# First four projection blocks run token block by token block, with matmuls on zeros before the first ones

## The chip, the cores and the metric

The kernel runs on one core of a Trainium2 chip. A core has five engines, each with its own instruction stream that it works off in program order: TensorE (PE, matrix products; its weight loads are listed as PEld), VectorE (DVE), ScalarE (ACT), GpSimd (POOL) and SyncE (SP, which here only issues DMA transfers and waits before them where the data isn't ready). Matmuls write to PSUM; everything else is in SBUF or in DRAM. The metric is the device time of the core in microseconds (us).

## The reference

```python
def mha(x, wqkv, wo):                       # x: 1 x 2048 x 512, 32 heads of 16
    q, k, v = split_heads(x @ wqkv)         # wqkv: 512 x 1536
    p = softmax(einsum("bhqd,bhkd->bhqk", q, k) * 16 ** -0.5)
    o = einsum("bhqk,bhkd->bhqd", p, v)
    return merge_heads(o) @ wo              # wo: 512 x 512

x = A_x
g = sigmoid((x * gate_w).sum(-1, keepdims=True))
return g * mha(x, A_wqkv, A_wo) + (1 - g) * mha(x, B_wqkv, B_wo)
```

Two attention blocks work on the same x with weights of their own, and a gate for each token mixes their results. Everything is float32.

## The kernel before

The kernel has a prologue, which projects x to queries, keys and values of both attention blocks, and a main loop over 64 heads (32 of each), which computes scores, exponentials and weighted sums. The change is in the prologue alone.

**The projection of queries and keys.** x comes in transposed (`xT`, 512 features by 2048 tokens) and is loaded in four token blocks of 512 (`load_x`). Each is split into a high and a low part in the format float32r (`split_x`: a cast on ACT to `xh`, a subtraction on DVE to `xl`). There are 16 projection blocks, `blocks`: for each attention block and each of four groups of eight heads, one for the queries and one for the keys, with weights of 512 x 128. A block's weights are loaded by `load_w` into one of three `wraw` buffers and split by `split_w` like x (`whi`, `wlo`, two buffers each). A product is then three products of parts (high by high, low by high, high by low) of four matmuls each: 12 matmuls for a block and 512 tokens, each 128x128 by 128x512.

**`project_qk`** takes one block and goes over two halves of 1024 tokens. A half is 24 matmuls into one of two PSUM tiles `ps_pro`; ACT then copies the result out as the high part `part0`, DVE makes the low part `part1` by a subtraction, and two stores on SP write them to DRAM (`qd` or `kd`). For a block of keys the difference of the first two blocks of 512 keys is computed on POOL too, split and stored (`key_difference`). After each half `between()` may put in score matmuls of the first heads.

**The order.** It is written out by hand: every engine gets its instructions in the order in which the Python code names them. At the start (lines 276 to 283) come the weights of block 0 and the first token block of x in four pieces, both are split, and then token blocks 1 to 3 are loaded and split in two pieces each, with the loads of the weights of blocks 1 and 2 between. The loop over the blocks (lines 296 to 311) splits the weights of the next block, issues the load of the weights of the block three further on, loads the value weights at block 2 and splits them at block 4, and projects. Then, at block 7, the values of the first attention block are projected (`project_v`), and later the heads' stacks of queries and keys are loaded back from DRAM (`load_stacks`).

SP issues all the transfers of the prologue but the load of the values; a store whose data isn't ready holds up the issues written behind it. ACT and DVE wait in the same way.

Of the kernel before, what the change touches and what calls it, by code (L numbers as in the profile page):

```python
# [23 lines left out]
F32 = mybir.dt.float32  # L24
F32R = mybir.dt.float32r
BF = mybir.dt.bfloat16
AF = mybir.ActivationFunctionType
ALU = mybir.AluOpType
# [4 lines left out]
P = 128  # L33
S = 2048
DM = 512
# [3 lines left out]
KC = DM // P  # L39
NQ = S // 512  # L40
# [7 lines left out]
HALVES = (0, 64)  # L48
SC = 3 * DH
KS = S + 512  # L50


@with_exitstack
def gated_mha(ctx: ExitStack, tc: tile.TileContext, xT, x, wqkv_a, wo_a, wqkv_b, wo_b, gate_w, out):
    nc = tc.nc
    pe, act, dve, pool = nc.tensor, nc.scalar, nc.vector, nc.gpsimd
# [6 lines left out]
    ps_m = ctx.enter_context(tc.tile_pool(name="ps_m", bufs=3, space=PSUM))  # L63

    qd = [[dram.tile([2, HG, DH, S], F32, name=f"qd{s}{g}") for g in range(NG)] for s in range(2)]
    kd = [[dram.tile([2, HG, DH, KS], F32, name=f"kd{s}{g}") for g in range(NG)] for s in range(2)]
    vd = [dram.tile([S, H * 17], F32, name=f"vd{s}") for s in range(2)]
# [112 lines left out]
    with tc.tile_pool(name="xs", bufs=1) as xs, tc.tile_pool(name="pro", bufs=2) as pro, \  # L180
            tc.tile_pool(name="ps_pro", bufs=2, space=PSUM) as ps_pro, \
            tc.tile_pool(name="ps_x", bufs=1, space=PSUM) as ps_x:
        xh = [xs.tile([P, KC, 512], F32R, name=f"xh{c}") for c in range(NQ)]
        xl = [xs.tile([P, KC, 512], F32R, name=f"xl{c}") for c in range(NQ)]
        wblocks = {}

        raws = {}

        def load_w(s, col, n):
            raw = pro.tile([P, KC, n], F32, name="raw" if n == 512 else "wraw", bufs=2 if n == 512 else 3)  # L190
            nc.sync.dma_start(raw, wqkv[s][:, col:col + n].rearrange("(k p) c -> p k c", p=P))
            raws[s, col] = raw

        def split_w(s, col, n):
            raw = raws.pop((s, col))
            tag, bufs = ("wv", 1) if n == 512 else ("w", 2)
            hi = pro.tile([P, KC, n], F32R, name=f"{tag}hi", bufs=bufs)
            lo = pro.tile([P, KC, n], F32R, name=f"{tag}lo", bufs=bufs)
            act.copy(hi, raw)
            dve.tensor_tensor(lo, raw, hi.bitcast(F32), op=ALU.subtract)  # L200
            wblocks[s, col] = (hi, lo)

        def load_x(c, n):
            raw = pro.tile([P, KC, 512], F32, name="raw")
            for k in range(0, KC, n):
                nc.sync.dma_start(raw[:, k:k + n], xT[k * P:(k + n) * P, c * 512:(c + 1) * 512].rearrange(
                    "(k p) t -> p k t", p=P))
            return raw

        def split_x(c, n, raw):  # L210
            for k in range(0, KC, n):
                act.copy(xh[c][:, k:k + n], raw[:, k:k + n])  # L212
                dve.tensor_tensor(xl[c][:, k:k + n], raw[:, k:k + n], xh[c][:, k:k + n].bitcast(F32),
                                  op=ALU.subtract)

        def key_difference(dst, parts):
            d = [pro.tile([P, 512], F32, name=f"kdiff{i}", bufs=1) for i in range(2)]
            for i in range(2):
                pool.tensor_tensor(d[i], parts[i][:, :512], parts[i][:, 512:], op=ALU.subtract)
            pool.tensor_tensor(d[0], d[0], d[1], op=ALU.add)  # L220
            hi = pro.tile([P, 512], F32R, name="kdiff_hi", bufs=1)
            lo = pro.tile([P, 512], F32R, name="kdiff_lo", bufs=1)
            pool.tensor_copy(hi, d[0])
            pool.tensor_tensor(lo, d[0], hi.bitcast(F32), op=ALU.subtract)
            for i, t in enumerate((hi, lo)):
                nc.sync.dma_start(dst[i].rearrange("h d t -> (h d) t")[:, S:], t.bitcast(F32))

        def project_qk(s, g, isk, between):
            hi, lo = wblocks.pop((s, isk * DM + g * P))
            dst = (kd if isk else qd)[s][g]  # L230
            for half in range(2):
                ps = ps_pro.tile([P, 1024], F32, name="ps_pro")
                for c in range(2):
                    cc = half * 2 + c
                    n = 0
                    for a, b in ((hi, xh[cc]), (lo, xh[cc]), (hi, xl[cc])):
                        for k in range(KC):
                            pe.matmul(ps[:, c * 512:(c + 1) * 512], a[:, k], b[:, k],  # L238
                                      start=n == 0, stop=n == 3 * KC - 1)
                            n += 1  # L240
                pt = [pro.tile([P, 1024], F32R, name=f"part{i}") for i in range(2)]
                act.copy(pt[0], ps)  # L242
                dve.tensor_tensor(pt[1], ps, pt[0].bitcast(F32), op=ALU.subtract)  # L243
                for i in range(2):
                    nc.sync.dma_start(dst[i].rearrange("h d t -> (h d) t")[:, half * 1024:(half + 1) * 1024],
                                      pt[i].bitcast(F32))
                if isk and half == 0:
                    key_difference(dst, [t.bitcast(F32) for t in pt])
                between()

        v_st = [const.tile([P, H, 17], F32, name=f"v_st{i}") for i in range(2)]
        for t in v_st:
            pool.memset(t[:, :, 16:17], 1.0)

        def project_v(s, t):
            hi, lo = wblocks[s, 2 * DM]
            c, o = divmod(t * P, 512)
            last = s == 1 and t == NT - 1
            ps = ps_m.tile([P, 512], F32, name="ps_m") if last else ps_pro.tile([P, 1024], F32, name="ps_pro")
            n = 0  # L260
            for a, b in ((xh[c], hi), (xl[c], hi), (xh[c], lo)):
                for k in range(KC):
                    pe.matmul(ps[:, :DM], a[:, k, o:o + P], b[:, k], start=n == 0, stop=n == 3 * KC - 1)  # L263
                    n += 1
            v = ps[:, :DM].rearrange("p (h d) -> p h d", h=H)
            act.copy(v_st[t % 2][:, :, 0:16], v)  # L266
            nc.sync.dma_start(vd[s][t * P:(t + 1) * P, :], v_st[t % 2].rearrange("p h d -> p (h d)"))

        blocks = [(s, g, isk) for s in range(2) for g in range(NG) for isk in range(2)]

        def block(fn, i):
            if i < len(blocks):
                s, g, isk = blocks[i]
                fn(s, isk * DM + g * P, P)

        block(load_w, 0)
        x0 = load_x(0, 1)
        block(split_w, 0)
        split_x(0, 1, x0)
        for c in range(1, NQ):  # L280
            split_x(c, 2, load_x(c, 2))
            if c < 3:
                block(load_w, c)
        ahead = [(m, part) for m in range(NT + LEAD) for part in range(NQ)]

        def run_ahead(n):
            turn[0] = 0
            for _ in range(n):
                m, part = ahead.pop(0)
                max_part(m, part, ps_x if part == NQ - 1 else None)  # L290
                if (m, part) == (NT - 1, NQ - 1):
                    max_split(0)
                    pending.append(0)

        pending = []
        for i, (s, g, isk) in enumerate(blocks):
            block(split_w, i + 1)
            block(load_w, i + 3)
            if i in (2, 8):
                load_w(i // 8, 2 * DM, DM)  # L300
            if i in (4, 9):
                split_w(i // 8, 2 * DM, DM)
            project_qk(s, g, isk, lambda: run_ahead((i >= 10) + 2 * (i >= 13)))
            if i in (5, 6, 8, 9):
                load_stacks(i // 8, HALVES[(i - 5) % 3:][:1])
            if i == 7:
                for t in range(NT):
                    project_v(0, t)
            if i == 9:
                for c in range(4):  # L310
                    load_v(0, c)
        for t in range(NT):
            project_v(1, t)
            if pending:
                pending[0] += 1
                if pending[0] == 3:
                    max_rows(pending.pop() - 3)
            if t and t != NT - 2:
                run_ahead(4)
        assert not ahead and not pending  # L320
# [233 lines left out]
    pt = {}  # L554
# [70 lines left out]
    for r in range(0, ROUNDS, 2):  # L625
        h, kt = divmod(r, NT)
# [10 lines left out]
        scored, parts = 0, 2  # L637
# [62 lines left out]
```

## Time and profile before

| | us |
|---|---|
| time before, median of the runs | 2811.56 |
| lowest of the runs | 2810.78 |
| the profiled execution's own time | 2810.61 |
| its span, from the first to the last instruction | 2808.8 |
| PE busy | 2789.1 |
| ACT busy | 2416.8 |
| DVE busy | 2397.4 |
| first real matmul starts at | 5.65 |
| projection block 1 starts at | 24.78 |

Rows of the profile name the line of the kernel, the engine, the operation, the tile written and the tiles read with their shapes (partitions x elements). In a list in order of time the first two numbers are the start and the duration in us, "x4" says that four instructions are merged into the row, and the brackets hold the idle time of the engine ahead of it and what ended it. A merged row of pipelined matmuls runs into the next one by the latency of the last, so the pace is read from the starts. A row for a stretch of time lists the length, the busy time of PE, PEld, DVE, ACT and POOL with the number of instructions, the granted clock of TensorE as a share of full speed, the busy share of the 16 DMA engines, and GB/s. "SPq" is an issue of a transfer by SP, not the transfer.

### The profile page before, as it was taken

How to read it: one execution, taken by the hardware profiler on the slowest of the kernel's cores; microseconds unless marked ns; L12 is line 12 of the kernel's file. 1: busy time of each engine (PE TensorE's matmuls, PEld its weight loads, DVE VectorE, ACT ScalarE, POOL GpSimd, SP SyncE). 2: the span in 40 equal slices, each digit the busy share in tenths (PEclk: the TensorE clock that was granted, in tenths of full speed). 3: DMA queues.
4: the chain of work that ended last, by engine and by line, in shares of the span. 5: the costliest groups of instructions: out<-in, count | busy, mean ns of one | idle time of the engine just before them, and what ended most of it. 6: DMA issues, size and time to landing. Idle time of an engine off the chain costs nothing.

```text
span 2808.8 us, 65084 instructions
## 1 busy us (share of the span) xinstructions
PE 2789.1 (99%) x26016; PEld 1429.3 (51%) x26016; DVE 2397.4 (85%) x4395; ACT 2416.8 (86%) x4755; POOL 280.2 (10%) x473
## 2 busy tenths in 40 slices
PE   8999999999999999999999999999999999999999
PEld 6877544444444444444444455544444444445544
DVE  3135899999999999999999878899999999998884
ACT  3221799999999999999999977899999999998785
POOL 3121132000000000000100231000000000011201
PEclk9999999999999999999999999999999999999999
DMA  7683433333333233333432442332333343333302
GB/s 254 208 252 145 93 80 86 56 61 62 73 65 57 52 61 62 60 63 61 92 56 51 107 93 74 61 59 51 65 58 61 62 80 72 57 76 91 77 11 93
DMA packets 86086, 231.62 MB, mean 82 GB/s; under 512 B 22134, under 2 KB 32342, under 8 KB 73238
## 3 DMA queue, kind: packets, MB, share of 16 engines
q1 hardware_dynamic: 83222, 218.53, 35.3%
q0 software_dynamic: 2560, 8.91, 1.2%
q8 instruction: 205, 3.36, 0.5%
q14 instruction: 99, 0.81, 0.1%
HBM read 158.46 MB, written 68.94 MB: 81 GB/s over the span
## 4 chain that ended last, share of the span: by engine, by line
PE 96%; DMA 2%; DVE 1%; SPq 1%; ACT 0%; issue 0%; POOL 0%; DVEq 0%; ACTq 0%
PE acc L566 38%; PE ps_st L615 31%; PE ps_m L124 14%; PE ps_pro L238 5%; PE ps_m L450 3%; PE ps_pro L263 3%; PE ps_st L124 1%; DMA qd<-part 1%; DMA raw<-in_xT 1%; DMA q_st<-qd 0%; DVE mxp L130 0%; DMA rb<-rd 0%; DMA vd<-v_st 0%; PE ps_st L450 0%; PE ps_st L501 0%
## 5 line engine op out<-in xcount | busy, mean ns | idle before, releaser
L617 ACT ACTIVATE p<-ps_st 128x512 f32<-128x512 f32 x4061 | 2131.0, 628 | 132.4 <-PE ps_m L124 71.4
L130 DVE TENSOR_REDUCE mxp<-ps_m 128x1 f32<-128x512 f32 x3072 | 1977.0, 684 | 150.5 <-PE ps_m L124 69.7
L615 PE MATMUL ps_st<-q_st,k_st 50*128 50x512 f32 x4061 | 1353.9, 438 | 0.3 <-ACT excess L139 0.3
L124 PE MATMUL ps_m<-k_st,q_st 48*128 48x512 f32 x3574 | 1265.4, 444 | 1.3 <-DVE mxp L130 0.7
L566 PE MATMUL acc<-p,vg 128*17 128x256 f32 (+2 forms) x16208 | 1187.5, 386 | 3.0 <-DVE ev L574 2.0
L615 PEld LDWEIGHTS ps_st<-q_st,k_st 50*128 50x128 f32 x4061 | 675.0, 184 | 379.6 <-ACT p L617 227.7
L124 PEld LDWEIGHTS ps_m<-k_st,q_st 48*128 48x128 f32 x3574 | 602.3, 184 | 365.1 <-DVE mxp L130 327.1
L566 PEld LDWEIGHTS acc<-p,vg 128*17 128x17 f32 x16208 | 322.7, 96 | 530.4 <-issue 404.4
L146 DVE CUSTOM_DVE_ANT_0 excess<-ps_m,excess 128x512 f32<-128x512 f32 x502 | 341.9, 681 | 0.0
L139 ACT ACTIVATE excess<-ps_st 128x512 f32<-128x512 f32 x502 | 300.7, 599 | 1.2 <-DVE mxp L130 1.2
L155 POOL CAST mparts<-mrow 128x16 fp32r<-128x16 f32 x64 | 12.6, 196 | 2038.1 <-DVE mrow L154 2038.1
L124 PE MATMUL ps_st<-k_st,q_st 48*128 48x512 f32 x502 | 205.2, 409 | 0.0
L242 ACT CAST part<-ps_pro 128x1024 fp32r<-128x1024 f32 x32 | 32.5, 1015 | 133.1 <-PE ps_pro L238 103.7
L243 DVE TENSOR_TENSOR part<-ps_pro,part 128x1024 fp32r<-128x1024 f32 x32 | 39.2, 1225 | 111.1 <-ACT part L242 92.2
L124 PEld LDWEIGHTS ps_st<-k_st,q_st 48*128 48x128 f32 x502 | 92.1, 183 | 0.2 <-issue 0.2
L450 PE MATMUL ps_m<-wo,ot 128*128 128x512 f32 (+1 forms) x354 | 90.7, 401 | 0.0
L266 ACT COPY v_st<-ps_pro 128x512 f32<-128x512 f32 x31 | 18.2, 587 | 79.5 <-PE ps_pro L263 73.7
L238 PE MATMUL ps_pro<-xh,whi 128*128 128x512 f32 x256 | 72.6, 402 | 9.9 <-ACT xh L212 9.1
L450 PEld LDWEIGHTS ps_m<-wo,ot 128*128 128x128 f32 (+1 forms) x354 | 64.0, 188 | 21.1 <-DVE mxp L146 6.8
L238 PE MATMUL ps_pro<-xh,wlo 128*128 128x512 f32 x256 | 69.4, 393 | 0.0
L238 PE MATMUL ps_pro<-xl,whi 128*128 128x512 f32 x256 | 69.1, 392 | 0.0
L238 PEld LDWEIGHTS ps_pro<-xh,whi 128*128 128x128 f32 x256 | 47.4, 190 | 25.1 <-ACT xh L212 11.7
(105 smaller groups left out, 902.3 us busy)
## 6 DMA issues: line engine op xcount, KB each, us to landing
k_st<-kd SPq DMA_DIRECT2D x128, 320.0 KB
q_st<-qd SPq DMA_DIRECT2D x128, 256.0 KB
k_st<-kd SPq DMA_DIRECT2D x128, 160.0 KB
qd<-part SPq DMA_DIRECT2D x32, 512.0 KB
kd<-part SPq DMA_DIRECT2D x32, 512.0 KB
q_st<-qd SPq DMA_DIRECT2D x128, 128.0 KB
od<-ev SPq DMA_DIRECT2D x63, 256.0 KB
vd<-v_st SPq DMA_DIRECT2D x32, 272.0 KB
```

Source lines behind the costliest of these rows:

```text
L124: pe.matmul(ps, q[b:b + SC, t * P:(t + 1) * P], k[b:b + SC, c * 512:(c + 1) * 512], start=True, stop=True)
L130: dve.tensor_reduce(mxp[h][:, t, part:part + 1], ps, op=ALU.max, axis=AX.X)
L139: act.activation(excess[m], ps, AF.Relu)
L146: dve.tensor_tensor_reduce(e, ps, e, 1.0, LOWEST, ALU.add, ALU.max, mxp[h][:, t, 1:2])
L238: pe.matmul(ps[:, c * 512:(c + 1) * 512], a[:, k], b[:, k], start=n == 0, stop=n == 3 * KC - 1)
L242: act.copy(pt[0], ps)
L243: dve.tensor_tensor(pt[1], ps, pt[0].bitcast(F32), op=ALU.subtract)
L263: pe.matmul(ps[:, :DM], a[:, k, o:o + P], b[:, k], start=n == 0, stop=n == 3 * KC - 1)
L450: pe.matmul(ps, ot[a][:n, slot, sl], wt[b][:n, g], start=G == groups[0] and i == 0, stop=G == groups[-1] and i == 2)
L566: pe.matmul(acc[32 * c:32 * c + 17, qa * P:qb * P], v[:, 4 * a + c if final else kt, j], p[:, c * 512 + qa * P:c * 512 + qb * P], start=fi ...
L615: pe.matmul(ps, k[b:b + SC + 2, kk * P:(kk + 1) * P], q[b:b + SC + 2, cc * 512:(cc + 1) * 512], start=True, stop=True)
L617: act.activation(pt[r][:, c * 512:(c + 1) * 512], ps, AF.Exp, scale=SCALE)
```

## The change

`FIRST = 4`: the first four blocks (queries and keys of the first two groups of heads of the first attention block) are no longer projected one after the other. The kernel goes over the four token blocks of x, and in each it projects blocks 0 and 1 into the two halves of one PSUM tile, then blocks 2 and 3. Their split weights stay in SBUF (four buffers for two). The other 12 blocks are projected as before, each in two halves of two token blocks.

The weights of blocks 1 and 2 are loaded between token blocks 0 and 1 of x, those of block 3 behind token block 1; the loads of blocks 4, 5 and 6, and the split of block 4, stand behind the four projected blocks. The value weights are loaded at block 4 and split at block 5. Token block c + 2 of x is loaded and token block c + 1 split after the first pair of token block c. The stores of a pair are four of 512 columns each where there were two of 1024. The key difference is now made from two calls, one for each of the token blocks 0 and 1.

Ahead of each of the first four real matmuls stand 10, 5, 3 and 6 matmuls on a tile of zeros in bf16, into a PSUM tile that is not read.

```diff
-            tag, bufs = ("wv", 1) if n == 512 else ("w", 2)
+            tag, bufs = ("wv", 1) if n == 512 else ("w", FIRST)
...
+        zeros = pro.tile([P, 512], BF, name="zeros", bufs=1)
+        dve.memset(zeros, 0.0)
+        idle = [6, 3, 5, 10]
+
+        def keep_warm():
+            if idle:
+                ps = ps_m.tile([P, 512], F32, name="ps_m")
+                for _ in range(idle.pop()):
+                    pe.matmul(ps, zeros[:, :P], zeros, start=True, stop=True)
+
+        def project(ps, w, c):
+            hi, lo = w
+            n = 0
+            for a, b in ((hi, xh[c]), (lo, xh[c]), (hi, xl[c])):
+                for k in range(KC):
+                    keep_warm()
+                    pe.matmul(ps, a[:, k], b[:, k], start=n == 0, stop=n == 3 * KC - 1)
+                    n += 1
+
+        def project_qk(todo):
+            ps = ps_pro.tile([P, 1024], F32, name="ps_pro")
+            for o, (i, c) in enumerate(todo):
+                s, g, isk = blocks[i]
+                project(ps[:, o * 512:(o + 1) * 512], wblocks[s, isk * DM + g * P], c)
+            pt = [pro.tile([P, 1024], F32R, name=f"part{i}") for i in range(2)]
+            act.copy(pt[0], ps)
+            dve.tensor_tensor(pt[1], ps, pt[0].bitcast(F32), op=ALU.subtract)
+            whole = todo[0][0] == todo[1][0]
+            for o, (i, c) in enumerate(todo):
+                s, g, isk = blocks[i]
+                dst = (kd if isk else qd)[s][g]
+                cols = slice(o * 512, (o + 1 + whole) * 512)
+                if not (whole and o):
+                    for p in range(2):
+                        nc.sync.dma_start(
+                            dst[p].rearrange("h d t -> (h d) t")[:, c * 512:(c + 1 + whole) * 512],
+                            pt[p][:, cols].bitcast(F32))
+                if isk:
+                    key_difference(dst, c, [t[:, o * 512:(o + 1) * 512].bitcast(F32) for t in pt])
...
         block(load_w, 0)
-        x0 = load_x(0, 1)
+        xr = {0: load_x(0, 1)}
+        for i in range(1, 3):
+            block(load_w, i)
+        xr[1] = load_x(1, 2)
         block(split_w, 0)
-        split_x(0, 1, x0)
-        for c in range(1, NQ):
-            split_x(c, 2, load_x(c, 2))
-            if c < 3:
-                block(load_w, c)
+        split_x(0, 1, xr[0])
+        block(load_w, 3)
+        for c in range(NQ):
+            for o in range(0, FIRST, 2):
+                if c == 0:
+                    for i in range(o, o + 2):
+                        if i:
+                            block(split_w, i)
+                project_qk([(o, c), (o + 1, c)])
+                if o == 0 and c + 1 < NQ:
+                    if c + 2 < NQ:
+                        xr[c + 2] = load_x(c + 2, 2)
+                    split_x(c + 1, 2, xr[c + 1])
+        for i in range(FIRST, FIRST + 3):
+            block(load_w, i)
+        block(split_w, FIRST)
...
-        for i, (s, g, isk) in enumerate(blocks):
+        for i in range(FIRST, len(blocks)):
             block(split_w, i + 1)
             block(load_w, i + 3)
-            if i in (2, 8):
+            if i in (4, 8):
                 load_w(i // 8, 2 * DM, DM)
-            if i in (4, 9):
+            if i in (5, 9):
                 split_w(i // 8, 2 * DM, DM)
-            project_qk(s, g, isk, lambda: run_ahead((i >= 10) + 2 * (i >= 13)))
+            for half in range(2):
+                project_qk([(i, 2 * half), (i, 2 * half + 1)])
+                run_ahead((i >= 10) + 2 * (i >= 13))
```

More of the change, by code (lines that the diff above doesn't have):

```diff
@@ L50 @@
 KS = S + 512
+FIRST = 4
 @with_exitstack
@@ L214, in split_x, with store_difference @@
                                   op=ALU.subtract)
[L216 to L220, printed above, removed]
+        def store_difference(dst, d):
             hi = pro.tile([P, 512], F32R, name="kdiff_hi", bufs=1)
             lo = pro.tile([P, 512], F32R, name="kdiff_lo", bufs=1)
-            pool.tensor_copy(hi, d[0])
-            pool.tensor_tensor(lo, d[0], hi.bitcast(F32), op=ALU.subtract)
+            pool.tensor_copy(hi, d)
+            pool.tensor_tensor(lo, d, hi.bitcast(F32), op=ALU.subtract)
@@ L225, in key_difference @@
             for i, t in enumerate((hi, lo)):
                 nc.sync.dma_start(dst[i].rearrange("h d t -> (h d) t")[:, S:], t.bitcast(F32))
[L228 to L249, printed above, removed]
@@ new lines, in gated_mha, with key_difference @@
+        kdiff = {}
+        def key_difference(dst, c, parts):
+            if c == 0:
+                d = kdiff[id(dst)] = pro.tile([P, 512], F32, name="kdiff")
+                pool.tensor_tensor(d, parts[0], parts[1], op=ALU.add)
+            elif c == 1:
+                d = kdiff.pop(id(dst))
+                for p in parts:
+                    pool.tensor_tensor(d, d, p, op=ALU.subtract)
+                store_difference(dst, d)
+        zeros = pro.tile([P, 512], BF, name="zeros", bufs=1)
@@ L276, in gated_mha @@
         block(load_w, 0)
-        x0 = load_x(0, 1)
+        xr = {0: load_x(0, 1)}
+        for i in range(1, 3):
+            block(load_w, i)
+        xr[1] = load_x(1, 2)
         block(split_w, 0)
-        split_x(0, 1, x0)
-        for c in range(1, NQ):
-            split_x(c, 2, load_x(c, 2))
-            if c < 3:
-                block(load_w, c)
+        split_x(0, 1, xr[0])
+        block(load_w, 3)
+        for c in range(NQ):
+            for o in range(0, FIRST, 2):
+                if c == 0:
+                    for i in range(o, o + 2):
[9 more added lines that the diff above has]
+        block(split_w, FIRST)
         ahead = [(m, part) for m in range(NT + LEAD) for part in range(NQ)]
```

## The prediction

> **What bounds the kernel now.** I read the page's busy table first, then the chain that ended last, then the groups by line, and then the first 60 us in order of time, because the diff touches nothing else.
>
> ```profile
> PE 2789.1 (99%) x26016; PEld 1429.3 (51%) x26016; DVE 2397.4 (85%) x4395; ACT 2416.8 (86%) x4755; POOL 280.2 (10%) x473
> PE 96%; DMA 2%; DVE 1%; SPq 1%; ACT 0%; issue 0%; POOL 0%; DVEq 0%; ACTq 0%
> L238 PE MATMUL ps_pro<-xh,whi 128*128 128x512 f32 x256 | 72.6, 402 | 9.9 <-ACT xh L212 9.1
> ```
>
> The first line gives each engine's busy time: TensorE (PE) has work for 99% of 2808.8 us. The second is the chain: 96% of it is PE. The third is the group of the projection's matmuls: in all 16 blocks PE sat idle before them for only 9.9 us, 9.1 of it for the split pieces of x. So the change plays for a few microseconds of 2810; about 2%, some 56 us, is what a measurement of this kernel can tell from no change. Whatever PE gains or loses here is kept, because PE stays the chain afterwards.
>
> The start, PE alone (start, duration, engine, line, count; in brackets the idle time before it and what ended it):
>
> ```profile
> 5.65 0.80 PE L238 MATMUL ps_pro<-xh,whi 128*128 128x512 f32 x1 [5.65 <-ACT xh L212]
> 10.26 0.80 PE L238 MATMUL ps_pro<-xh,whi 128*128 128x512 f32 x1 [1.30 <-ACT xh L212]
> 10.86 1.91 PE L238 MATMUL ps_pro<-xh,wlo 128*128 128x512 f32 x4
> 12.56 1.74 PE L238 MATMUL ps_pro<-xl,whi 128*128 128x512 f32 x4
> 14.14 1.08 PE L238 MATMUL ps_pro<-xh,whi 128*128 128x512 f32 x4
> 16.88 0.61 PE L238 MATMUL ps_pro<-xh,whi 128*128 128x512 f32 x2
> 18.03 0.72 PE L238 MATMUL ps_pro<-xh,whi 128*128 128x512 f32 x2 [0.54 <-ACT xh L212]
> 21.79 0.73 PE L238 MATMUL ps_pro<-xh,whi 128*128 128x512 f32 x2 [0.65 <-ACT xh L212]
> 24.78 1.20 PE L238 MATMUL ps_pro<-xh,whi 128*128 128x512 f32 x4 [0.43 <-DVE part L243]
> 25.82 1.07 PE L238 MATMUL ps_pro<-xh,wlo 128*128 128x512 f32 x4
> 59.37 0.84 PE L238 MATMUL ps_pro<-xl,whi 128*128 128x512 f32 x3
> ```
>
> From 25.82 to 59.37 lie 37 groups of four: 33.55 / 148 = 0.2267 us a matmul, the full pace. A pair of (block, 512 tokens) is 24 of them, 5.44 us; a block is 10.88. From 10.26 to 14.14 nine matmuls take 3.88 us instead of 2.04: the slow start costs 1.84. From 16.88 to 24.78 the last 24 matmuls of block 0 take 7.90 instead of 5.44: waits cost 2.46. Block 4 starts at 24.78 + 3 x 10.88 = 57.42. So 1.84 + 2.46 = 4.30 us is all that the change can win from 10.26 on, 0.15% of the time; the fourth piece of x, split at 10.24, is where both kernels must wait.
>
> **Part 1: matmuls on zeros.** 24 matmuls on zeros stand before the first four real ones (10, 5, 3, 6). PE can start at about 1.1 us: it is released with ScalarE (ACT), whose first row begins at 0.73, and needs one short memset on VectorE (DVE), which is idle until 4.41.
>
> ```profile
> 0.73 1.28 ACT L199 ACT_TABLE_LOAD   x1 [0.73 <-PEq L689]
> 4.41 0.69 DVE L200 TENSOR_TENSOR wlo<-wraw,whi 128x512 fp32r<-128x512 f32 x1 [4.41 <-ACT whi L199]
> ```
>
> No matmul of this shape in bf16 is in the trace; the nearest are the float32r ones of 512 columns, 0.43 us slow (1.74 / 4) and 0.2267 fast. Ten slow ones end at 5.4, just as the first piece is ready (5.65). Then 14 and three real ones need 17 x 0.2267 = 3.9 us if the pace has risen, and end at 9.5, before 10.26: free. All slow they need 7.3 and end at 13.0, 2.7 late. In the trace 3.88 us of steady work lifted the pace, so I take 0 and keep 2.7 for the range. The gain is the 1.84 above: the pair (blocks 0 and 1, tokens 0 to 511) ends at 10.26 + 21 x 0.2267 = 15.02. The weights of block 1 now go ahead of the second 512 tokens, so they do not hold it up.
>
> **Part 2: token block by token block.** The 24 matmuls of 16.88 to 24.78 no longer wait for x, a gain of 2.46, if the next pair can start. It cannot at once. Every engine works in program order, and so here:
>
> ```profile
> 11.11 1.05 ACT L212 CAST xh<-raw 128x1024 fp32r<-128x1024 f32 x1 [0.90 <-DMA raw<-in_xT]
> 12.46 1.05 ACT L212 CAST xh<-raw 128x1024 fp32r<-128x1024 f32 x1 [0.31 <-DMA raw<-in_xT]
> 20.69 1.05 ACT L212 CAST xh<-raw 128x1024 fp32r<-128x1024 f32 x1 [0.34 <-DMA raw<-in_xT]
> 21.64 0.62 ACT L199 CAST whi<-wraw 128x512 fp32r<-128x512 f32 x1
> 22.16 1.01 ACT L242 CAST part<-ps_pro 128x1024 fp32r<-128x1024 f32 x1
> 21.77 1.23 DVE L213 TENSOR_TENSOR xl<-raw,xh 128x1024 fp32r<-128x1024 f32 x1 [0.16 <-ACT xh L212]
> 22.91 0.68 DVE L200 TENSOR_TENSOR wlo<-wraw,whi 128x512 fp32r<-128x512 f32 x1
> 23.51 1.22 DVE L243 TENSOR_TENSOR part<-ps_pro,part 128x1024 fp32r<-128x1024 f32 x1
> ```
>
> The eviction at 22.16 is of a half that PE had finished before 16.88; it waited on ACT behind the splits written ahead of it. In the changed program the weights of blocks 2 and 3 are split after project_qk of the first pair, and after split_x(1). So on ACT there stand, behind an eviction that must wait for PE at 15.02: the eviction 1.01, two pieces of x 2 x 1.05, the high part of block 2's weights 0.62, together 3.73, with hand-offs 3.9. PE waits for that last one: 3.9 us idle. On DVE stand 1.22 + 2 x 1.23 + 0.68 behind the first 1.01: 5.37, with hand-offs 5.6; the low weights therefore come 5.6 after 15.02, when PE, after four matmuls (0.91), has waited 0.8 more. Sum of **stall 1**: 4.7 us. The x pieces are not later than that: they had landed by 11.1 and 12.5, and two weight blocks of 0.25 MB now ahead of them put the second off by 0.5 / 0.228 = 2.2 us, to 14.7 (last column, GB/s):
>
> ```profile
> 10.00:15.00 5.00, 4.74 (x13) 3.79 (x14) 3.14 (x3) 2.30 (x3) 0.82 (x5) 1.00 0.77 228
> ```
> First four blocks: 15.02 + 4.7 + 168 x 0.2267 = 57.8, against 57.42. The order of work gives back what it wins: +0.4.
>
> Stores of those blocks are halved in size and doubled in number, 32 for 16. An issue takes about 0.32 on the queue of SyncE (SP), four in each 5.44 us, hidden, except in Part 3. The key difference stays three sums per block on GpSimd, and only SP waits for it; x's last block, queued behind one, is needed about 10 us later.
>
> **Part 3: the loads of blocks 4 to 6.** Before, weights were loaded three blocks ahead. Now they are written after the stores of the last pair, which SP works off in order:
>
> ```profile
> 23.20 3.80 SPq L245 DMA_DIRECT2D qd<-part  x4
> 27.05 0.63 SPq L191 DMA_DIRECT2D wraw<-in_wqkv_a  x1
> 36.27 0.32 SPq L226 DMA_DIRECT2D kd<-kdiff_hi  x1
> 0.74 0.46 SPq L191 DMA_DIRECT2D wraw<-in_wqkv_a  x1
> 3.76 0.62 ACT L199 CAST whi<-wraw 128x512 fp32r<-128x512 f32 x1 [1.75 <-DMA wraw<-in_wqkv_a]
> 30.00:31.00 1.00, 1.00 (x6) 0.84 (x5) 0.00 (x0) 0.45 (x1) 0.00 (x0) 1.00 0.89 202
> 31.00:32.00 1.00, 1.00 (x6) 0.81 (x5) 0.40 (x1) 0.57 (x1) 0.35 (x1) 1.00 0.27 76
> ```
>
> (The last two rows are stretches of one microsecond; their last columns are the clock, the DMA share and GB/s.) Let PE end the last pair at T. The eviction and the subtraction end at T + 2.4; three more stores take SP to T + 3.5; then the load of block 4's weights is issued. With nothing ahead of it a load took from 0.74 to 3.76, 3.02 us, to its split; behind four stores of 0.5 MB, issued at 27.05, the queue ran until about 31.3, 4.3 us and some landing. Here half as many bytes stand ahead: T + 6.5 to T + 8.0, then 0.62 for the split. Nothing else is there for PE, whose next matmul is block 4's; on ACT and DVE only block 5's split stands behind. **Stall 2**: 7.2 to 8.6, and I take 7.4, nearer the empty queue, as most stores have left by then.
>
> **Part 4: the pace after each stall.** The trace shows the clock fall once:
>
> ```profile
> 302.50 0.49 PE L124 MATMUL ps_m<-k_st,q_st 48*128 48x512 f32 x1 [0.67 <-DVE mxp L130]
> 113.57 1.20 PE L263 MATMUL ps_pro<-wvhi,xh 128*128 128x512 f32 x4 [1.45 <-ACT v_st L266]
> 113.00:120.00 7.00, 6.43 (x28) 5.36 (x29) 0.00 (x0) 2.28 (x4) 0.00 (x0) 1.00 0.31 121
> 303.00:306.00 3.00, 2.72 (x9) 1.16 (x9) 3.00 (x8) 2.11 (x5) 0.16 (x1) 0.68 1.16 163
> 306.00:309.00 3.00, 3.00 (x22) 0.98 (x24) 1.75 (x4) 2.41 (x5) 0.00 (x0) 0.50 0.91 183
> 309.00:312.00 3.00, 3.00 (x28) 1.29 (x22) 1.73 (x4) 1.58 (x3) 0.00 (x0) 0.68 0.96 115
> ```
>
> The granted clock was half for 0.64 x 3 + 3 + 0.64 x 3 = 6.8 us, which loses 3.4, after a stretch in which 0.67 us was the longest idle time but the matmuls were thin (48 rows). An idle time of 1.45 between full ones at 113.57 left it at 1.00. The start of the kernel, idle and then sparse, lost 1.84. Stall 2 is like the start: 1.84 to 3.4, I take 2.4. Stall 1 is between the cases: 0, or 1.84 to 3.4 less the 0.8 that the wait for low weights hides; I take 1.0 and keep 0 to 2.6.
>
> [...]
>
> **The sum.** +0.4 (gain 4.3, stall 1 4.7) + 1.0 + 7.4 + 2.4 = +11.2 us. From block 5 on each load and split is again ahead of its use, and the waits at 113.57 and 302.50 come with the work, only later. On the profiled execution's 2810.61 this is 2821.8. The median shown, 2811.56, is 0.95 above that; I say **2822**, 0.4% slower, which cannot be told from no change by the 2% above. Its own range: 0.4 + 0 + 7.2 + 1.8 = 9.4 gives 2820; 0.4 + 2.6 + 8.6 + 3.4 + 2.7 = 17.7 gives 2828. Chance 66%; 5% more for the clock's fall at 303 coming or not coming again, plus or minus 3.4.
>
> **The rivals.** *Both stalls are covered*: if the splits of blocks 2 to 4 come early enough, the 4.3 stays: 2806.9. For it, the 9.9 idle shows the gain is there; against it, the order on ACT at 22.16 and on SP at 27.05. 10%. *Only stall 1*: the weights of block 4 are there in time; 2811.0 to 2813.6 by 0.4 to 3.0 on top. It needs SP to pass its stores, which no row shows. 9%. *The zeros do not lift the clock*: the change does not do what it says; matmuls on zeros end late by 2.7 and the slow start of 1.84 is back: 2826.3. 7%. [...] 3%.
>
> Range for 8 in 10: from stall 1 alone to the forecast's upper end, 2811 to 2828. Faster by over 2% would need 56 us where 4.3 are to be had: 1%. Slower: 3%. Within: 96%.
>
> **What would show it.** In the changed profile: full pace before 10.26 and the first pair's end at about 15; an idle time of about 3.9 before block 2's first matmul, ended by ACT's split of weights, and 0.8 before its low weights; no wait for x up to the last pair's end, near 58 to 59; then 7 us or more ended by the split of block 4's weights, itself waiting for the load; slow matmuls behind it; the main loop unchanged. A row without that second idle time, or a main loop of another length, would prove me wrong.

## The result, and the profile after

The changed kernel takes 2828.44 us, median of 6 runs (2827.12 to 2829.17). The kernel before takes 2811.56 beside it, the median of five runs without one slow one of 4107.17. The ratio is 1.006, 95% interval 1.005 to 1.007. So it is slower by 16.9 us: less than the 2% that were set for a difference, but clear of the noise, which is about 0.1% here and not the 2% that the prediction took for it. The direction and both stalls were forecast, the size was not: the forecast was 2822, and the measured time lies 0.4 us above the top of its range, 2828.

The page of the changed kernel: span, busy time, engines of the chain, the group of the projection's first product with the idle time before it.

```profile
span 2825.3 us, 65151 instructions
PE 2800.4 (99%) x26040; PEld 1434.8 (51%) x26040; DVE 2401.2 (85%) x4396; ACT 2417.1 (86%) x4755; POOL 283.1 (10%) x473
PE 97%; DMA 1%; DVE 1%; ACT 0%; issue 0%; SPq 0%; POOL 0%; ACTq 0%; POOLq 0%; DVEq 0%
L253 PE MATMUL ps_pro<-xh,whi 128*128 128x512 f32 x256 | 73.0, 406 | 12.1 <-ACT whi L200 11.3
```

(The span is 16.5 us longer.) The idle time before the projection grew only from 9.9 to 12.1 us, and what ends it now is the split of weights, 11.3 of it, instead of the split of x. PE's busy time grew by 11.3 us: it holds the matmuls on zeros, and matmuls that ran slower. The first 76 us, PE in order of time:

```profile
1.19 4.08 PE L245 MATMUL ps_m<-zeros 128*128 128x512 bf16 x10 [1.19 <-DVE zeros L238]
12.19 1.07 PE L253 MATMUL ps_pro<-xh,whi 128*128 128x512 f32 x4
14.01 1.07 PE L253 MATMUL ps_pro<-xl,whi 128*128 128x512 f32 x4
18.59 2.08 PE L253 MATMUL ps_pro<-xh,whi 128*128 128x512 f32 x4 [3.51 <-ACT whi L200]
21.39 2.08 PE L253 MATMUL ps_pro<-xh,wlo 128*128 128x512 f32 x4 [0.72 <-DVE wlo L201]
24.97 1.22 PE L253 MATMUL ps_pro<-xh,whi 128*128 128x512 f32 x4
59.59 1.07 PE L253 MATMUL ps_pro<-xl,whi 128*128 128x512 f32 x4
68.44 2.07 PE L253 MATMUL ps_pro<-xh,whi 128*128 128x512 f32 x4 [7.77 <-ACT whi L200]
73.41 1.09 PE L253 MATMUL ps_pro<-xh,whi 128*128 128x512 f32 x4
```

The first pair ends at 14.01 + 4 x 0.2267 = 14.92, and both forecast stalls are there: block 2 starts 3.67 us after that, and block 4 starts 7.94 us after 60.50, where the fourth block ends. What ACT did before block 2, and SP and ACT before block 4, is the order that the prediction had followed: two pieces of x ahead of block 2's weights, and the last stores ahead of block 4's load.

```profile
16.02 1.99 ACT L213 CAST xh<-raw 128x1024 fp32r<-128x1024 f32 x2
17.91 1.14 ACT L200 CAST whi<-wraw 128x512 fp32r<-128x512 f32 x2
63.37 0.91 SPq L271 DMA_DIRECT2D kd<-part  x2
64.33 5.18 SPq L192 DMA_DIRECT2D wraw<-in_wqkv_a  x4
67.77 0.62 ACT L200 CAST whi<-wraw 128x512 fp32r<-128x512 f32 x1 [6.05 <-DMA wraw<-in_wqkv_a]
```

Behind each stall the matmuls are slow: 2.08 for four instead of 1.07. The granted clock says why (columns as before; the clock is third from the end):

```profile
18.00:21.00 3.00, 2.08 (x4) 1.17 (x4) 3.00 (x3) 1.05 (x3) 1.64 (x1) 0.57 0.89 287
60.00:63.00 3.00, 0.66 (x3) 0.20 (x2) 1.23 (x1) 1.01 (x1) 0.00 (x0) 0.96 0.33 125
69.00:73.00 4.00, 4.00 (x11) 3.10 (x10) 0.80 (x2) 0.48 (x1) 0.00 (x0) 0.50 0.65 206
125.00:128.00 3.00, 0.31 (x2) 0.00 (x0) 0.00 (x0) 0.44 (x1) 0.00 (x0) 0.94 0.75 295
128.00:131.00 3.00, 2.80 (x7) 2.25 (x8) 0.00 (x0) 0.73 (x2) 0.00 (x0) 0.50 0.50 185
316.00:319.00 3.00, 1.98 (x8) 0.74 (x7) 2.82 (x6) 3.00 (x7) 2.60 (x3) 0.96 0.97 221
319.00:323.00 4.00, 4.00 (x19) 1.70 (x19) 3.14 (x7) 3.02 (x6) 0.00 (x0) 0.50 1.03 150
329.00:332.00 3.00, 3.00 (x38) 1.37 (x36) 2.52 (x5) 3.00 (x7) 1.29 (x1) 1.00 0.24 90
```

Before there was one fall of the clock, at the start of the main loop, for 6.8 us. Now there are four, and the one at the main loop's start lasts about 10.2; behind it the clock rows show no other. The third, near 128, belongs to a wait that the prediction had only moved along, in the projection of the values:

```profile
114.25 1.07 PE L289 MATMUL ps_pro<-wvhi,xh 128*128 128x512 f32 x4
128.20 2.08 PE L289 MATMUL ps_pro<-wvhi,xh 128*128 128x512 f32 x4 [2.89 <-ACT v_st L292]
132.37 1.09 PE L289 MATMUL ps_pro<-wvhi,xh 128*128 128x512 f32 x4
```

Before, the same wait was 1.45. So the loss, by points of the work that both traces have (start of the same instruction after, less before):

| point | before | after | difference |
|---|---|---|---|
| block 4 | 57.42 | 68.44 | 11.0 |
| first value tile (12 slow matmuls behind the second stall) | 101.07 | 114.25 | 13.2 |
| last thin matmuls before the main loop | 298.22 | 313.72 | 15.5 |
| end of the span | 2808.8 | 2825.3 | 16.5 |

### The profile page after: what moved, and what is told of

The parts are those of the page before. It is cut to its first block, busy times and chain, and to the rows that moved or that the text cites. A ratio compares the mean times of both kernels' runs of the same rounds, so it can differ in the third digit from the quotient of the medians.

```text
span 2825.3 us, 65151 instructions
## 1 busy us (share of the span) xinstructions
PE 2800.4 (99%) x26040; PEld 1434.8 (51%) x26040; DVE 2401.2 (85%) x4396; ACT 2417.1 (86%) x4755; POOL 283.1 (10%) x473
## 4 chain that ended last, share of the span: by engine, by line
PE 97%; DMA 1%; DVE 1%; ACT 0%; issue 0%; SPq 0%; POOL 0%; ACTq 0%; POOLq 0%; DVEq 0%
PE acc L608 38%; PE ps_st L657 31%; PE ps_m L125 14%; PE ps_pro L253 6%; PE ps_m L492 3%; PE ps_pro L289 3%; PE ps_st L125 1%; DMA q_st<-qd 0%; DVE mxp L131 0%; DMA vd<-v_st 0%; PE ps_st L492 0%; PE ps_st L543 0%; DMA raw<-in_xT 0%; PE ps_m L657 0%; PE ps_m L543 0%
## 5 line engine op out<-in xcount | busy, mean ns | idle before, releaser
L253 PE MATMUL ps_pro<-xh,whi 128*128 128x512 f32 x256 | 73.0, 406 | 12.1 <-ACT whi L200 11.3
L253 PEld LDWEIGHTS ps_pro<-xh,whi 128*128 128x128 f32 x256 | 48.3, 193 | 26.7 <-ACT whi L200 12.1
```

The source lines that it names most:

```text
L253: pe.matmul(ps, a[:, k], b[:, k], start=n == 0, stop=n == 3 * KC - 1)
```

## The experiments

Each run is timed against the kernel before on the same chip (its medians there: 2810.6, 2810.2 and 2809.9 for the three groups of four). The groups ran on different chips, so two versions are compared by their ratios to the kernel before; where the intervals of two ratios overlap, the times alone don't tell the two apart, and the rows of their traces decide. Unless it says otherwise an edit is to the changed kernel. Theory: PE waits twice because of where splits and loads stand in the order, and each wait costs clock as well; what came on top later (3.2 us) is a value store issued later because of the key difference. Rivals: the DMA engines, through smaller stores; and the matmuls on zeros.

**Loads of blocks 4 to 6 earlier.**

```diff
                     split_x(c + 1, 2, xr[c + 1])
-        for i in range(FIRST, FIRST + 3):
-            block(load_w, i)
-        block(split_w, FIRST)
+                if o == 0 and c == 2:
+                    for i in range(FIRST, FIRST + 3):
+                        block(load_w, i)
+                if o == 0 and c == 3:
+                    block(split_w, FIRST)
```

> The loads of the weights of blocks 4 to 6 go behind the first pair of token block 2, the split of block 4 behind the first pair of token block 3; nothing else differs from the changed kernel. Theory (PE waited 7.94 us at block 4 for a load queued on SP behind the last stores, then ran 12 matmuls at half clock): the idle time at block 4 goes, block 4 starts at 60.5 and runs at full pace, 7.9 + 2.3 = 10.2 us less, about 2818. Rival (the smaller stores clog the DMA engines, so the load is late wherever it is issued): the idle time stays at 3 us or more, 2822 or more.

Measured 2817.91 us, ratio 1.0025 (1.0015 to 1.0034). Expected 2818. The trace has no idle time in that place, and full pace past the fourth block's end (four matmuls start every 0.91 us):

```profile
60.09 1.07 PE L253 MATMUL ps_pro<-xl,whi 128*128 128x512 f32 x4
61.00 1.07 PE L253 MATMUL ps_pro<-xh,whi 128*128 128x512 f32 x4
```

So the second stall was the load's place in SP's order. The stores, still of half size, did not hold it up.

**Splits of blocks 2 and 3 earlier.**

```diff
-                if c == 0:
-                    for i in range(o, o + 2):
-                        if i:
-                            block(split_w, i)
+                if c == 0 and o == 0:
+                    block(split_w, 1)
+                    block(split_w, 2)
                 project_qk([(o, c), (o + 1, c)])
+                if c == 0 and o == 0:
+                    block(split_w, 3)
```

> Weights of block 2 are split before the first pair is projected, those of block 3 directly behind it, ahead of the split of token block 1; nothing else differs from the changed kernel. Theory (at 14.92 PE waited for splits behind an eviction and two pieces of x, 3.67 us, then ran at half clock and waited 0.72 more; 12 matmuls took 6.38 for 2.72): block 2 starts at about 15 at full pace, 3.67 + 3.66 = 7.3 us less, about 2821. Rival (the weights themselves land late): an idle time of 2 us or more stays, ended by a load.

Measured 2819.92, ratio 1.0033 (1.0021 to 1.0045); expected 2821. The second pair follows the first without a wait, here at 14.44:

```profile
13.53 1.07 PE L253 MATMUL ps_pro<-xl,whi 128*128 128x512 f32 x4
14.44 1.07 PE L253 MATMUL ps_pro<-xh,whi 128*128 128x512 f32 x4
```

The weights had landed; only their split stood too late.

**Both.** The two edits together.

> Both edits of the first two runs. Theory: the two stalls add up, the first four blocks end near 53 and block 4 follows at once, 17.5 us less than the changed kernel on this stretch: 2811, and 4.4 less than the kernel before up to block 4. What is left of the difference later (3.2 us: a longer wait in the value projection and more half clock) decides whether it ends at 2807 (nothing left) or 2811 (all left). Rival (part of the time returns as another wait in the first 60 us): block 4 starts at 57 or later.

Measured 2810.71, ratio 0.9998 (0.9989 to 1.0007). The first value tile starts at 96.14, 4.9 us ahead of the kernel before, as expected (4.4, and x was 0.6 earlier in this run). None of it reaches the end: the span is 2809.1. The wait in the value projection stands in the way, with slow matmuls behind it, and the clock falls at the main loop's start for 10.2 us, and once more near 2773.

```profile
110.42 2.07 PE L289 MATMUL ps_pro<-wvhi,xh 128*128 128x512 f32 x4 [3.22 <-ACT v_st L292]
2772.00:2777.00 5.00, 5.00 (x28) 1.18 (x25) 0.00 (x0) 3.15 (x7) 1.28 (x1) 0.66 0.00 0
```

**The key difference in its old order** (for the blocks projected whole).

```diff
+        def whole_difference(dst, parts):
+            d = [pro.tile([P, 512], F32, name="kdiff") for i in range(2)]
+            for i in range(2):
+                pool.tensor_tensor(d[i], parts[i][:, :512], parts[i][:, 512:], op=ALU.subtract)
+            pool.tensor_tensor(d[0], d[0], d[1], op=ALU.add)
+            store_difference(dst, d[0])
...
-                if isk:
+                if isk and whole:
+                    if c == 0:
+                        whole_difference(dst, [t.bitcast(F32) for t in pt])
+                elif isk:
                     key_difference(dst, c, [t[:, o * 512:(o + 1) * 512].bitcast(F32) for t in pt])
```

> Only the key difference of the blocks projected whole (block 5 on) is computed as in the kernel before: subtraction of the high parts first, which need only the eviction on ACT, then of the low parts, then the sum. Theory (the new order begins with a sum that waits for DVE's low part, 1.3 us later, and SP, waiting for it, issues the value stores later, so that PE waits 3.05 us instead of 1.61 near 128 and the clock falls for 3.4 us): the wait is back near 1.6, the clock stays, 1.4 + 1.3 = 2.7 us less, about 2826. Rival (the wait is longer because more transfers are queued ahead, whatever the key difference does): it stays near 3, 2828.

Measured 2823.05, ratio 1.0045 (1.0028 to 1.0062) where the changed kernel has 1.006 (1.005 to 1.007): the times alone don't tell the two apart, so the rows must. The span is 5.0 us less, 2820.3. Both stalls are still there. The wait in the value projection is down to 0.90, lower than in the kernel before, and the clock stays full behind it. First the changed kernel's GpSimd and SP rows, then those of this run, then its wait:

```profile
112.31 1.29 POOL L230 TENSOR_TENSOR kdiff<-part,part 128x512 f32<-128x512 f32 x1 [16.63 <-DVE part L263]
117.11 1.28 POOL L221 TENSOR_TENSOR kdiff_lo<-kdiff,kdiff_hi 128x512 fp32r<-128x512 f32 x1
119.80 13.76 SPq L293 DMA_DIRECT2D vd<-v_st  x5
```

```profile
109.91 2.60 POOL L240 TENSOR_TENSOR kdiff<-part 128x512 f32<-128x512 f32 x2 [15.74 <-ACT part L269]
114.62 1.29 POOL L221 TENSOR_TENSOR kdiff_lo<-kdiff,kdiff_hi 128x512 fp32r<-128x512 f32 x1
117.74 15.03 SPq L303 DMA_DIRECT2D vd<-v_st  x6
126.01 1.20 PE L299 MATMUL ps_pro<-wvhi,xh 128*128 128x512 f32 x4 [0.90 <-ACT v_st L302]
```

With the new order the first sum waits for DVE's low part instead of ACT's eviction, the key difference ends 2.5 us later, and the first value store is issued 2.1 us later. That is the same number of sums on an engine that is 10% busy. By the last thin matmuls before the main loop (310.31 against 313.72) 3.4 us of the 5.0 between the two spans are this; the other 1.6 come from the fall of the clock at the main loop's start, which lasts 6.8 us here and 10.2 in the changed kernel, and at which the edit didn't aim.

**Both stalls removed and the old key difference.**

> Both edits that removed the two stalls, and the key difference in its old order. Theory (the 4.4 us that the order of the projection wins were given back by the wait in the value projection, 3.2 us near 110, and the half clock behind it): that wait falls below 1.6, no half clock near 110, and the time is 3 us below the run with both edits alone, about 2807.5, less what the half clock at the start of the main loop happens to last. Rival (the gain is lost at the main loop's start whatever comes before): 2810 to 2811.

Measured 2806.57, ratio 0.9986 (0.9976 to 0.9995): faster than the kernel before, by 0.14%. The first value tile starts at 96.18, the wait behind it is 0.95, the clock stays full there, and the span is 2803.8, 5.0 less than before. Now the gain of the order arrives at the end (some 4.3 us; the last piece of x was 0.7 earlier too). The ratio's interval overlaps that of the run before it (0.9989 to 1.0007); by the first score matmul behind the last value tile (294.08 against 296.91) the old order is worth 2.8 of the 5.3 us between those two spans. The rest are shorter falls of the clock in the main loop (6.8 us at its start, where that run has 10.2 there and 3.4 near 2773), at which no edit aimed.

**The same without the matmuls on zeros.**

```diff
-        idle = [6, 3, 5, 10]
+        idle = []
```

> As the run before it, but without the 24 matmuls on zeros. Theory: from 10.26 on nine matmuls run slow again and x's later pieces are not waited for; the first pair ends 1.8 us later, at 16.9, and the whole is 1.8 us longer. Rival (the zeros hold the first real ones up by as much as they win): no difference.

Measured 2807.24, ratio 0.9989 (0.9980 to 0.9999), not told apart from the run with zeros. The expected 1.8 us were too much: here x's last piece was ready earlier, and the pace rose between 11.13 and 12.19 instead of after 12.56, so that the slow start was shorter; the first value tile starts only 0.34 later (96.52). In this run the wait in the value projection was 2.33 with a clock of 0.53 behind it, which makes the rest of the 2.5 us between the spans. So the old order of the key difference doesn't guarantee a short wait: here GpSimd's second subtraction itself had to wait 0.53 us for DVE's low part, and the first value store was issued 1.6 us later than in the run with zeros (101.68 for 100.08).

```profile
6.34 3.29 PE L260 MATMUL ps_pro<-xh,whi 128*128 128x512 f32 x4 [6.34 <-ACT xh L213]
9.43 1.91 PE L260 MATMUL ps_pro<-xh,wlo 128*128 128x512 f32 x4
11.13 1.22 PE L260 MATMUL ps_pro<-xl,whi 128*128 128x512 f32 x4
```

**The kernel before with the zeros alone.**

```diff
+        zeros = pro.tile([P, 512], BF, name="zeros", bufs=1)
+        dve.memset(zeros, 0.0)
...
                         for k in range(KC):
+                            keep_warm()
                             pe.matmul(ps[:, c * 512:(c + 1) * 512], a[:, k], b[:, k],
```

> The kernel before with the 24 matmuls on zeros alone. Theory: the first 24 real matmuls end 1.8 us earlier, but the next 24 wait for x as before (21.79 is set by a piece of x), so nearly all of it is lost again: block 1 starts at 24.8, no difference, 2810.6. Rival (the faster start carries on): 2809 or less.

Measured 2810.44, ratio 1.0000 (0.9991 to 1.0009). Block 1 starts at 24.68 for 24.78: the faster start ends in a longer wait for x, 1.19 where 0.65 was.

```profile
21.68 0.73 PE L249 MATMUL ps_pro<-xh,whi 128*128 128x512 f32 x2 [1.19 <-ACT xh L212]
24.68 1.20 PE L249 MATMUL ps_pro<-xh,whi 128*128 128x512 f32 x4 [0.43 <-DVE part L254]
```

**Zeros in the two stalls.**

```diff
         idle = [6, 3, 5, 10]
+        stalls = {(2, 0): 14, (FIRST, 0): 32}
...
+                if (i, c) in stalls:
+                    idle.append(stalls.pop((i, c)))
                 project(ps[:, o * 512:(o + 1) * 512], wblocks[s, isk * DM + g * P], c)
```

> The changed kernel with 14 more matmuls on zeros before block 2's first and 32 before block 4's first, so that PE is not idle in its two stalls (3.67 and 7.94 us, which stay). Theory (part of the loss is the half clock after each, 2.9 us and 2.3 us): the matmuls behind the stalls run at full pace, about 5 us less, 2823.5; the waits for splits stay. Rival (the clock falls whatever PE did, or the zeros end late): less than 2 us.

Measured 2824.56, ratio 1.0054 (1.0037 to 1.0071): by the time alone it can't be told from the changed kernel's 1.006, and theory and rival can't be told apart. The rows can: the waits for the splits stay, and the clock does not fall in them or behind them (1.00 in 18 to 25 and in 60 to 73; the last row is a part of that):

```profile
18.34 1.20 PE L254 MATMUL ps_pro<-xh,whi 128*128 128x512 f32 x4 [0.47 <-ACT whi L200]
21.16 1.19 PE L254 MATMUL ps_pro<-xh,wlo 128*128 128x512 f32 x4 [1.62 <-DVE wlo L201]
23.11 1.08 PE L254 MATMUL ps_pro<-xh,whi 128*128 128x512 f32 x4
69.00:73.00 4.00, 4.00 (x19) 3.34 (x18) 0.00 (x0) 0.64 (x1) 0.00 (x0) 1.00 0.88 309
```

This parts wait from clock. Block 2's 12 matmuls take 4.77 here, 6.38 in the changed kernel and 2.72 at full pace: 2.05 of waiting for the low weights and starting again (1.62 of it idle time), 1.6 of clock. The first value tile starts 4.0 us earlier than in the changed kernel (110.24 for 114.25). The span keeps 2.6 of that, 2822.7, as the wait in the value projection is 3.56 here, with half pace behind it (1.92 for four, 1.07 ahead of it).

**Four value tiles** instead of two, in the prologue's memory.

```diff
-        v_st = [const.tile([P, H, 17], F32, name=f"v_st{i}") for i in range(2)]
+        v_st = [pro.tile([P, H, 17], F32, name=f"v_st{i}", bufs=1) for i in range(4)]
...
-            act.copy(v_st[t % 2][:, :, 0:16], v)
+            act.copy(v_st[t % 4][:, :, 0:16], v)
...
```

> The changed kernel with four result tiles for the value projection instead of two (in the prologue's memory), so that the projection of a tile no longer waits for the store of the one two before it. Theory (the wait near 128 is for those stores, queued late on SP): no idle time there and no half clock behind it, 3.05 + 1.3 = 4.4 us less, 2824; the two stalls before stay. Rival (the stores are so late that four tiles only put the wait off): a wait of 2 us or more some microseconds later.

Measured 2823.52, ratio 1.0046 (1.0031 to 1.0060); expected 2824. PE does not wait in the value projection at all, and there is no half pace there (four matmuls start every 0.91 us from 114.19 on): the wait was for the stores. (Of the 5.7 us between the spans, 2819.6 and 2825.3, some 1.7 are again the fall at the main loop's start, 6.8 us here.)

**All of these: both stalls removed, the old key difference, four value tiles.**

> Both stalls removed, the key difference in its old order, and the four value tiles. Theory: the run without the four tiles still had 1.1 us of that wait, so about 1 us less than its 2806.6, 2805.5. Rival (waits for the queue just move on): no difference, or the next wait grows.

Measured 2804.82, ratio 0.9980 (0.9971 to 0.9990), 0.2% under the kernel before: the lowest of the versions run, though not told apart from the 0.9986 without the four tiles. Once the first pair has begun, PE waits only 0.26 us up to the last value tile. The rival came true in part: at the main loop's start the clock falls for 10.2 us again, and a new wait of 1.2 stands there, behind the landing of a value store (the first row is from the chain of waits): the value tiles' memory passes to the main loop.

```profile
291.94 2.07 DMA vd<-v_st
294.77 0.79 PE L670 MATMUL ps_st<-q_st,k_st 50*128 50x512 f32 x1 [1.21 <-ACT excess L140]
```

**Zeros at the main loop's start**, on top of that (the tile of zeros is moved to memory that outlives the prologue).

```diff
...
                 score(r + scored // 4, scored % 4)
                 scored += 1
+                if r == 0:
+                    pe.matmul(acc, zeros[:, :P], zeros, start=True, stop=True, skip_group_check=True)
```

> As the run before it, with eight matmuls on zeros among the scores of the main loop's first two rounds (into the accumulator, ahead of its first use), where PE idles 0.3, 0.3 and 0.7 us and the clock has fallen for 6.8 us or more in every run. [...]

Measured 2813.20, ratio 1.0011 (1.0001 to 1.0020), 8 us longer than the run before it. It doesn't show whether such matmuls can keep the clock up: the first zero matmul had to wait 1.73 us for the clearing of the accumulator on DVE, and behind that wait the pace was at half for longer, about 13.6 us, from the matmul at 296.66 to the one at 310.24 (10.2 in the run before it). The mean granted clock of the whole span is 0.997 (0.998 in the run before it). The 1.73 us and the longer stretch don't add up to the whole 8 us; the rest is open.

```profile
295.17 0.39 PE L699 MATMUL acc<-zeros 128*128 128x512 bf16 x1 [1.73 <-DVE acc L388]
```

**The kernel before with the new key difference alone.**

```diff
...
-            for i in range(2):
-                pool.tensor_tensor(d[i], parts[i][:, :512], parts[i][:, 512:], op=ALU.subtract)
-            pool.tensor_tensor(d[0], d[0], d[1], op=ALU.add)
...
+            pool.tensor_tensor(d[0], parts[0][:, :512], parts[1][:, :512], op=ALU.add)
+            for p in parts:
+                pool.tensor_tensor(d[0], d[0], p[:, 512:], op=ALU.subtract)
```

> The kernel before with the changed order of the key difference alone (sum of the first token block's parts first, then two subtractions). Theory: the wait in the value projection, 1.6 us before, grows to about 3, with 1.3 us of half clock behind it if a window falls there: 2812 to 2813.5. Rival (the order does nothing by itself): 2810.5.

Measured 2813.15, ratio 1.0011 (1.0002 to 1.0020). The wait is 2.54 for 1.45, and the clock falls with it: 0.88 in 112 to 114, so half from 113.52 on, and 0.51 in 114 to 117. (What the expectation calls a window no run shows as such; the rows show falls that lie whole steps of 3.41 us apart, in the last section.) So this one edit, which the new order of blocks needs for the first four blocks only, costs about 3 us by itself, in both kernels (here 0.6 to 5.6 by the interval, and 3.4 by the rows of the changed kernel). All traces fit: with the new order of the sums the first value store is issued 5.3 to 6.2 us behind the start of the first value tile (seven traces), with the old one 3.7 to 4.4 (six), and 5.2 in the run without zeros. With two value tiles the wait is 2.54 to 3.56 with the new order (six traces) and 0.90 to 1.45 with the old (four), and 2.33 in the run without zeros.

```profile
114.01 2.07 PE L263 MATMUL ps_pro<-wvhi,xh 128*128 128x512 f32 x4 [2.54 <-ACT v_st L266]
114.00:117.00 3.00, 2.99 (x7) 2.41 (x8) 0.00 (x0) 0.59 (x1) 0.00 (x0) 0.51 0.49 188
```

## Why the prediction was right in kind and short by 5 us

| term of the sum | predicted | measured |
|---|---|---|
| end of the first pair | 15.02 | 14.92 |
| stall 1: weights of block 2, high and low | 4.7 | 5.7 (3.67 + 2.05) |
| clock behind stall 1 | 1.0 | 1.6 and 0.14 behind block 2 |
| stall 2: weights of block 4 | 7.4 | 7.94 |
| clock behind stall 2 | 2.4 | 2.3 |
| after block 4's start | 0 | 2.3 up to the main loop, 1.0 in it |
| sum, less the gain of 4.3 (4.4 measured) | 11.2 | 16.5 |

- **Part 1** (zeros): right, and by itself worth nothing (block 1 at 24.68 for 24.78 in the kernel before with zeros), as it only brings forward a wait for x. With both stalls removed it was worth 0.34 us at the first value tile, not 1.84.
- **Part 2** (stall 1): the mechanism was right, and moving the splits removed it. The mis-sized term is "PE, after four matmuls (0.91), has waited 0.8 more": it was 2.05 at full clock. The two pieces of x on DVE took 3.44 us, 1.7 each, where the prediction took 1.23 each. The new sum of the key difference ran on GpSimd at the same time; two pieces later in the same trace, with GpSimd idle (0.00 us busy in 48 to 51), took 2.55 (last row):

```profile
17.30 3.44 DVE L214 TENSOR_TENSOR xl<-raw,xh 128x1024 fp32r<-128x1024 f32 x2
17.47 2.18 POOL L230 TENSOR_TENSOR kdiff<-part,part 128x512 f32<-128x512 f32 x1 [6.59 <-DVE part L263]
48.23 2.55 DVE L214 TENSOR_TENSOR xl<-raw,xh 128x1024 fp32r<-128x1024 f32 x2 [1.47 <-ACT xh L213]
```

  The sum takes 1.29 at 112.31, where it runs alone. No run took the sum away from beside the pieces, so that it is the cause rests on this comparison. The prediction had named this sum and called it hidden, since nobody but SP waits for it; it didn't ask what would run beside it. Side by side DVE took 0.9 us longer than the 2.55 and GpSimd 0.9 longer than the 1.29. No run shows whether one of the two held up the other, or how.
- **Part 3** (stall 2): right; 7.94 lies between the bounds 7.2 and 8.6. The issue came 3.83 after the last matmul for 3.5, and the landing took 3.44 for 3.0 with an empty queue.
- **Part 4** (clock): right that both stalls cost clock; for stall 1 the term was 1.0, a choice between 0 and 2.6, and the runs showed 1.7. In all four versions that keep stall 1 without zeros in it (the changed kernel, early loads, old key difference, four tiles) the matmuls by the low weights behind it run at half pace, 2.07 to 2.08 for four (1.07 at full pace), so the 0 came in none of them.
- **The step that failed most**, a term put at 0 that measured 3.3: "From block 5 on each load and split is again ahead of its use, and the waits at 113.57 and 302.50 come with the work, only later." Loads and splits were ahead, but the wait of 1.45 became 2.89 and cost clock, 2.3 us up to the main loop. "Whatever PE gains or loses here is kept" failed with it: in the run with both edits PE was 4.9 us ahead at the first value tile, and nothing of it was left at the end. The cause is an edit that the prediction passed over with "three sums per block on GpSimd, and only SP waits for it". SP's next issues are the value stores, whose landing ACT and then PE wait for; the order of the three sums decided when SP came to them. The old order in the changed kernel and the new order in the kernel before show it from both sides. The other 1.0 lies in the main loop, with the longer fall at its start.
- **The sum and its range** were added to the profiled execution's 2810.61, not to the median 2811.56, though the forecast is of a median. As a difference 16.9 lies inside the stated 9.4 to 17.7. That is luck: the upper bound holds 2.7 us for zeros that end late, which did not happen, and nothing for what did happen behind block 4.
- The fall at the main loop's start came again, but for 10.2 us instead of 6.8; the prediction had a case for this, of plus or minus 3.4, and gave it 5%. Of the two falls, the longer one cost about 1.6 us more (the rows of the run with the old key difference).
- The rival "only stall 1" and the rival "zeros do not lift the clock" are refuted by the rows at 68.44 and 12.19. Slower by over 2%, with a chance of 3%, did not come: the ratio is 1.006, and the clock rows show no fall behind 329. The rival "both stalls are covered" is what the runs with both edits build. It priced them at 2806.9 (4.3 less than 2810.61 would be 2806.3); 2806.57 is measured once the key difference is back as well, 3.6 us less than the kernel before on that chip.

## What to carry to other kernels

When a diff changes the order of work, follow each in-order queue past the moved instruction, to the last waiter behind it: here two splits, one load and one order of three additions each stood one place too late, and in the prologue of these runs the idle waits of 2.33 to 8.01 us on TensorE behind the first pair (the two stalls and the value projection) were each followed by half pace. An operation on an idle engine isn't free if a queue waits for it and something else waits for that queue: the order of three sums on an engine that is 10% busy was worth 3.4 us here. And look for the gain at the end of the span, not at the end of the stage: 4.9 us won by 96 us were all gone by the end in one version and all there in another.

## What the runs showed of the hardware that was not expected

- **The changed kernel's four falls of the clock lie on a grid of 3.41 us, and each lasts whole steps of it.** Its clock rows give the moments: 0.57 in 18 to 21 means half clock for 2.58 us, so from 18.42 on; 0.96 in 60 to 63 gives 62.76, 0.94 in 125 to 128 gives 127.64, 0.96 in 316 to 319 gives 318.76. They lie 44.34, 64.88 and 191.12 us apart, which is 13, 19 and 56 times 3.413. They last 6.8, 10.2, 3.4 and 10.2 us, so two, three, one and three steps. In the run with zeros at the main loop's start the half pace lasts about 13.6, near four.
- **In the prologue the clock fell after 2.05 us of idle time and stayed up through 1.62.** Waits of 2.33 to 3.56 us in the value projection (seven traces) were each followed by half pace, waits of 0.90 to 1.45 in the same place (four traces) by none. In the kernel before with the new key difference the clock fell at 113.52 (0.88 in 112 to 114), when PE had been idle for 2.05 us, from 111.47 on. In the run with zeros in the stalls an idle time of 1.62 (19.54 to 21.16) left the clock at 1.00 in 18 to 25.
- **At the main loop's start the clock fell in every run**, behind idle times of at most 0.7 us and thin matmuls (48 and 50 rows) where the value tiles were as before; in the traces without a clock row there it is read from the pace, 0.79 us for a score matmul instead of 0.49. How long it stayed down goes with the moment of the fall, counted from the first score matmul behind the last value tile (314.51 in the changed kernel): 4.0 to 4.5 us behind it (five of those runs) it lasted 10.2, and 3.6 to 3.9 or 5.0 to 5.1 (six runs) 6.8. That it is a matter of where the grid falls on the work is a guess from these offsets. No run moved the work alone by a known amount to prove it, so this stays open. The difference is about 1.6 us of span, and any two spans compared here may hold it by chance.
- **DVE and GpSimd were both longer side by side**: 3.44 for 2.55 (two pieces of x) and 2.18 for 1.29 in the rows above, and so in the other versions with the new sum beside the split of x (3.45 for two pieces and 1.66 for the sum with both stalls removed).
